# A replicating store in place of three loads, and the first tile in four pieces

## The chip, the core and the metric

The kernel runs on one core of a Trainium2 chip. The metric is the device time of one execution in microseconds (us); the median of three runs stands for it. A core has a matrix engine (TensorE, PE in the profile; its weight loads are listed apart as PEld), three engines for elementwise work (VectorE or DVE, ScalarE or ACT, GpSimd or POOL) and SyncE (SP), which here only issues DMAs. DMAs issued by SP, ACT and POOL move data between HBM and the on-chip memory (128 partitions). Engines run on their own and wait for each other through semaphores.

## The reference

One transformer block in bfloat16 with 2048 tokens of width 1024. First, attention in which each token looks at eight earlier tokens, two apart; then a gated MLP that also mixes tokens.

```python
def _A_ref(x, wqkv, wo):                 # H = 32 heads of 32, W = 8 positions, dil = 2
    qkv = (x @ wqkv).reshape(B, S, 3, H, Dh).transpose(2, 0, 3, 1, 4)
    q, k, v = qkv[0], qkv[1], qkv[2]
    idx = pos[:, None] - off[None, :]    # off = 0, 2, ..., 14; masked where below 0
    logits = einsum('bhsd,bhswd->bhsw', q, k[idx]) * scale
    attn = softmax(where(mask, logits, -1e9))
    o = einsum('bhsw,bhswd->bhsd', attn, v[idx])
    return o.transpose(0, 2, 1, 3).reshape(B, S, D) @ wo

def _B_ref(x, w_in, w_sp, b_sp, w_out):  # Fh = 1792
    z = gelu(x @ w_in)
    z1, z2 = z[..., :Fh], layernorm(z[..., Fh:])
    g = einsum('ts,bsf->btf', w_sp, z2) + b_sp[None, :, None]
    return (z1 * g) @ w_out

h = x + _A_ref(layernorm(x), wqkv, wo)
out = h + _B_ref(layernorm(h), w_in, w_sp, b_sp, w_out)
```

## The kernel before

Tokens are taken in four chunks of 512, each of four tiles of 128 rows. The order is: q, k and v of all chunks; attention of each chunk with the output projection and the second layer norm ("head"); the two halves of the MLP input (`b_z2`, `b_z1`); and a last phase with the token mixing (L912) and the output projection (L927).

**The start.** Tiles 0 and 1 of x are loaded at L220 to L222, each in a left half (columns 0 to 511) issued by SP and a right half issued by ACT. Then ACT issues the load of `csb`, the constants, which hold the identity matrix that the transposes multiply with; SP goes on with the eight 256 KB pieces of the q weights (`wsb[0]`, "wq" in the profile), with tiles 2 and 3 in between, and later tiles and weights. Eight semaphores serve the DMAs of SP and ACT in turn, so a DMA can be issued only when the one eight before it has landed. Meanwhile TensorE runs `NWARM` matmuls on zeros (L211), whose result nobody uses. Tile 0 then goes through VectorE's statistics (`stats`, L240: one instruction per half), a square root on ACT, a reciprocal and three pieces of normalisation (L272). TensorE transposes the pieces (`xpose`, L283), ACT copies them out of PSUM (L284), and `q_left` (L287) begins with the products of tile 0 and the first five pieces of wq. Tile 1 follows on the same engines, then tiles 2 and 3. From the products of k and v on (L439), TensorE's work is large matmuls alone.

**The order of work.** PE, ACT, DVE and POOL execute in an order fixed at build time: the class `Order` plays through operations with estimated costs and priorities and emits them as it would start them. SP's instructions are ordered by the framework, outside the hand-written order (but for the first loads, L217). Costs in the planner are not touched by the change, and the planner knows a spread as one DMA operation of 7.0 us (`dma_op(7.0, spread, [prev])`).

**Attention.** In `attention(c)` (L461), partitions hold head and sub-dimension (p = 4 h + j, with 32 heads h and four j), and eight sub-steps `dl` lie in the free dimension. VectorE forms q*k for the eight positions and adds them up; TensorE sums over j, which gives logits in a layout of partition (q, h): a quarter q of the 512 tokens and a head. The softmax is done in that layout and gives `st["attn"]`, [128, 8 positions, 128 tokens]. To weigh v, every weight must be on all four partitions of its head: the tile `st["AB"]`. For positions 0 to 3 this is done by TensorE with a 0/1 matrix (`pbm`, L581, then copies at L594). For positions 4 to 7, "the second weight group", it goes through HBM (`spread`, L573): SP stores `attn[:, 4:8]` into `att_d[c]` (L574), and then loads it four times (L576), once for each j, into the partitions j, j+4, j+8, ... of AB. The first load must wait until the store has landed; what SP has to issue next stands behind it.

VectorE then multiplies v by the weights: y and z (positions 0 and 1), oT and zz (2 and 3), at L610, and position 4 as `av_b` at L613, the first that reads the second group; positions 5 to 7 as `av_p`, with additions (L621). y+z and oT+zz are added by DMAs that POOL issues (`gather`, L627; "av_y" and "av_oT"). The last addition completes `av_oT`, which the output projection reads as TensorE's stationary operand (L684).

**Other transfers near the spread.** SP stores q, k and v of later chunks from staging tiles (`stg`, four buffers, L451). POOL loads k, q, v of the next chunk (L470) and the MLP weights (`win`, L369).

Of the kernel before, what the change touches and what calls it, by code (L numbers as in the profile page):

```python
# [11 lines left out]
BF16 = mybir.dt.bfloat16  # L12
# [8 lines left out]
P = 128  # L21
NT = S // P
CH = 512
NCH = S // CH
# [5 lines left out]
EPS = 1e-5  # L30
SCALE = DH ** -0.5
NEG = -1.0e9
NWARM = 11
ALONE = 5
XRB = 3
LMODE = (1, 1, 1, 1)
# [27 lines left out]
class Order:  # L64
# [6 lines left out]
    def add(self, eng, us, fn, deps=(), prio=5.0, lat=0.1, take=None, free=None, table=None):  # L71
        o = _Op()
        o.eng, o.us, o.fn, o.prio, o.lat, o.free, o.table = eng, us, fn, prio, lat, free, table
        o.take = (take,) if isinstance(take, str) else take or ()
        o.deps = [d if isinstance(d, tuple) else (d, d.lat) for d in deps if d is not None]
        o.start, o.end, o.n = None, None, len(self.ops)
        self.ops.append(o)
        return o
# [49 lines left out]
def kernel(  # L128
# [12 lines left out]
    nc = tc.nc  # L141
    V, A, T = nc.vector, nc.scalar, nc.tensor
    dma = nc.sync.dma_start
    dma_w = nc.gpsimd.dma_start
    x2d = A_x[0]
# [6 lines left out]
    dpool = ctx.enter_context(tc.tile_pool(name="dram", bufs=1, space=DRAM))  # L152
    qkv_d = [dpool.tile([P, DLO, S], BF16, name=f"qkv_d{i}") for i in range(3)]
    h_d = dpool.tile([S, D], BF16, name="h_d")
    att_d = [dpool.tile([P, CH], BF16, name=f"att_d{i}") for i in range(NCH)]
    z1_d = dpool.tile([NF, P, S], BF16, name="z1_d")
    z2_d = dpool.tile([S, FH], BF16, name="z2_d")

# [36 lines left out]
    xts = {}  # L195
    pairs = {}

    def x_slot(i):
        if i // 2 not in pairs:
            pairs[i // 2] = l1.tile([P, 2, D], BF16, name="xp", tag="x4k", bufs=4)  # L200
        xts[i] = pairs[i // 2][:, i % 2, :]

    def load_pair(k):
        x_slot(2 * k)
        x_slot(2 * k + 1)
        dma(pairs[k][:], x2d[2 * k * P:(2 * k + 2) * P, :].rearrange("(t p) d -> p t d", p=P))
# [3 lines left out]
    wps = ps_tp.tile([P, CH], FP32, name="wps", tag="t0")  # L210
    for _ in range(NWARM):  # L211
        T.matmul(wps[:], warm[:, 0:P], warm[:], start=True, stop=True)
# [4 lines left out]
    with tc.manual_schedule(engines={mybir.EngineType.SP}):  # L217
        for i in range(TPC):
            x_slot(i)
        for i in range(2):  # L220
            for q_, lo in ((nc.sync, 0), (nc.scalar, CH)):
                q_.dma_start(xts[i][:, lo:lo + CH], x2d[i * P:(i + 1) * P, lo:lo + CH])  # L222
        A.dma_start(csb[:], consts_d.ap()[:, :])
        for kt in range(KT):
            dma(wsb[0][:, kt, :], wq_view[:, kt, 0:D])
            if kt == 4:
                for i in (2, 3):
                    dma(xts[i], x2d[i * P:(i + 1) * P, :])
        load_pair(2)
        load_pair(3)  # L230
        dma(wsb[1][:], wq_view[:, :, D:2 * D])
        load_pair(4)
        load_pair(5)
        xl = att.tile([P, TPC, D], BF16, name="xl", tag="prod", bufs=2)
        dma(xl[:], x2d[3 * CH:4 * CH, :].rearrange("(t p) d -> p t d", p=P))
        for i in range(TPC):
            xts[3 * TPC + i] = xl[:, i, :]
        dma(wsb[2][:], wq_view[:, :, 2 * D:3 * D])
# [137 lines left out]
    def dma_op(us, fn, deps, lat=0.1, free=None):  # L376
        return add("DMA", us, fn, deps, lat=lat, free=free)
# [83 lines left out]
    def attention(c):  # L461
# [18 lines left out]
        st, parts, qs, pvs = {}, {}, [{} for _ in range(W_WIN)], {}  # L480
# [5 lines left out]
        for g in range(W_WIN // nw):  # L486
            adds = []
            for wi in range(nw):
                w = g * nw + wi
# [53 lines left out]
        for hw in range(2):  # L543
            ws = slice(4 * hw, 4 * hw + 4)
# [20 lines left out]
        for hw in range(2):  # L565
            ws = slice(4 * hw, 4 * hw + 4)
            def at(ws=ws, hw=hw):
                if hw == 0:
                    st["AB"] = att.tile([P, W_WIN, CH], BF16, name="AB", tag="part", bufs=2)
                V.tensor_tensor(st["attn"][:, ws, :], st["sme"][:, 1, ws, :], st["rinv"][:].unsqueeze(1).to_broadcast([P, 4, P]), op=ALU.mult)  # L570
            prev = add("DVE", 0.61, at, [prev], prio=3.0, lat=0.1, take="part" if hw == 0 else None, free="prod" if hw else None)
            if hw:
                def spread(ws=ws):  # L573
                    dma(att_d[c][:], st["attn"][:, ws, :].rearrange("p w s -> p (w s)"))  # L574
                    for j in range(4):
                        dma(st["AB"][j::4, 4:8, :], att_d[c][:].rearrange("(q h) n -> h q n", h=32))  # L576
                abs_[1, 0] = abs_[1, 1] = dma_op(7.0, spread, [prev])
                break
            wait = add("DMA", BSLACK, lambda: None, [prev])
            for sh in range(2):  # L580
                def pbm(sh=sh, ws=ws, hw=hw):  # L581
                    if sh == 0:
                        pb = ps_att.tile([P, 2, 4, P], FP32, name="pb", tag="L")
                    else:
                        pb = ps_acc.tile([P, 2, 4, P], FP32, name="pba", tag="acc")
                    st["pb", hw, sh] = pb
                    for j in range(2):
                        sq = 2 * sh + j
                        T.matmul(pb[:, j], B4[32 * sq:32 * sq + 32, :], st["attn"][32 * sq:32 * sq + 32, ws, :],  # L589
                                 start=True, stop=True, tile_position=(32 * sq, 0))  # L590
                pm = add("PE", 0.20, pbm, [wait], prio=1.0, take="acc" if sh else "L", lat=0.2)
                eng = "DVE" if (hw == 0 and sh == 1) else "ACT"
                def cp(sh=sh, ws=ws, hw=hw, eng=eng):
                    (V.tensor_copy if eng == "DVE" else A.copy)(  # L594
                        st["AB"][:, ws, sh * 256:(sh + 1) * 256].rearrange("p w (j s) -> p j w s", j=2), st["pb", hw, sh][:])
                abs_[hw, sh] = add(eng, 1.25 if eng == "DVE" else 0.91, cp, [pm], prio=1.0 if eng == "ACT" else 2.9,
                                   free="acc" if sh else "L", lat=0.15)
# [304 lines left out]
    for c in range(NCH):  # L902
        wspT = wspTs[c]
        zg = p2.tile([P, NF, CH], BF16, name="zg", tag="zg")
        for fp in range(NF // 2):
# [3 lines left out]
            for j in range(2):  # L909
                f = 2 * fp + j  # L910
# [8 lines left out]
        for il in range(TPC):  # L919
            i = c * TPC + il  # L920
# [52 lines left out]
```

## Time and profile before

| | |
|---|---|
| median of three runs | 723.3 us (723.22 to 723.41) |
| profiled execution | 723.34 us, span of its records 721.6 us |
| granted TensorE clock, mean over the span | 1.00 |
| DMA moved | 113.12 MB, 157 GB/s over the span |
| landing of the store `att_d` (128 KB) | 1.7 to 2.4 us after issue |
| landing of a load of AB (128 KB) | 2.5 to 8.0 us after issue, slowest in chunk 1 |

In the profile a line such as "L613 DVE TENSOR_TENSOR av_b<-vT,AB" names the kernel's line, the engine, the operation and the tiles written and read. Views used here are: the page (a summary of the span), the waits (who waited for whom), the chain (the work that ended last, followed back), the timeline (start, duration, instruction and in brackets the idle time before it with what ended it), the view of one tile, and the DMA view, which for any stretch of time gives each queue's packets, MB and share of the engines' time. Queue q1 carries what SP issues, q10 what ACT issues, q0 what POOL issues. "Landing" is the time from the start of a DMA's issue to its last semaphore update.

### The profile page before, as it was taken

What the parts mean: (1) busy time and instruction counts of PE and PEld (TensorE: products, weight loads), DVE (VectorE), ACT (ScalarE), POOL (GpSimd) and SP (SyncE); (2) the same over time, 40 slices, a digit from 0 to 9 for tenths busy, and PEclk for the clock granted to TensorE, in tenths of its full rate; (3) what the DMA queues carried; (4) which work ended last, traced back from release to release, by engine and by line L of the source; (5) the groups of instructions that cost most, each with busy time, mean ns of one, the idle gap of its engine ahead of it and who ended that gap; (6) DMA issues with size and microseconds to landing.
All of it is one profiled execution on the core that took longest, in us unless ns stands there. A gap on an engine that the chain in (4) does not pass through costs nothing.

```text
span 721.6 us, 8559 instructions
## 1 busy us (share of the span) xinstructions
PE 714.1 (99%) x3493; PEld 370.3 (51%) x3537; DVE 420.8 (58%) x470; ACT 217.7 (30%) x280; POOL 51.2 (7%) x61
## 2 busy tenths in 40 slices
PE   8999999999999999999999999999999999999998
PEld 7766665666545444445445444444444444444444
DVE  6899899999999799988951103222222222222222
ACT  4523432533348866738825420000000000000000
POOL 0100010012110111000204100000000000000000
PEclk9999999999999999999999999999999999999999
DMA  9964697389973594642849899163016411120002
GB/s 327 322 185 110 201 215 206 128 233 277 312 301 58 188 238 142 233 117 66 223 129 294 230 299 295 48 148 116 29 45 128 132 33 45 35 86 11 0 17 71
DMA packets 117590, 113.12 MB, mean 157 GB/s; under 512 B 68080, under 2 KB 95120, under 8 KB 117424
## 3 DMA queue, kind: packets, MB, share of 16 engines
q1 hardware_dynamic: 108528, 75.48, 35.7%
q0 software_dynamic: 8448, 36.64, 17.6%
q8 instruction: 27, 0.44, 0.3%
q10 hardware_dynamic: 576, 0.47, 0.2%
q14 instruction: 11, 0.09, 0.0%
HBM read 57.19 MB, written 31.26 MB: 123 GB/s over the span
## 4 chain that ended last, share of the span: by engine, by line
PE 98%; DMA 0%; DVE 0%; issue 0%; ACT 0%
PE acc L912 27%; PE acc L439 21%; PE acc L816 13%; PE acc L761 13%; PE acc L927 13%; PE acc L684 8%; PE acc L287 2%; DMA xp<-in_A_x_dram 0%; PE L L527 0%; PE tpt L283 0%; PE pb L589 0%; DVE bnst L242 0%; DVE xn L272 0%; DVE bnst L243 0%; PE tpa L283 0%
## 5 line engine op out<-in xcount | busy, mean ns | idle before, releaser
L912 PE MATMUL acc<-wspT,z2sb 128*128 128x512 bf16 x878 | 193.1, 379 | 0.9
L912 PEld LDWEIGHTS <-z2sb 128*128 128x128 bf16 x896 | 87.7, 98 | 105.7
L915 DVE TENSOR_TENSOR g<-acc,bB 128x1024 bf16<-128x1024 f32 x28 | 34.3, 1224 | 160.2 <-PE acc L912 127.9
L816 PE MATMUL acc<-hnT,win 128*128 128x512 bf16 x448 | 98.0, 379 | 0.0
L761 PE MATMUL acc<-win,hnT 128*128 128x512 bf16 (+1 forms) x501 | 97.4, 352 | 0.6
L761 PEld LDWEIGHTS <-hnT 128*128 128x128 bf16 x512 | 49.9, 98 | 47.5 <-issue 0.7
L497 DVE TENSOR_TENSOR prod<-qT,kT 128x4096 bf16<-128x4096 bf16 x32 | 72.4, 2283 | 0.0
L927 PEld LDWEIGHTS <-zg 128*128 128x128 bf16 x462 | 44.7, 98 | 52.4
L816 PEld LDWEIGHTS <-win 128*128 128x128 bf16 x448 | 43.7, 98 | 52.6 <-issue 0.7
L450 ACT CAST stg<-acc 128x1024 bf16<-128x1024 f32 x36 | 36.4, 1011 | 77.2 <-PE acc L439 66.4
L934 DVE TENSOR_TENSOR ot<-acc,hr 128x1024 bf16<-128x1024 f32 x15 | 18.4, 1225 | 69.4 <-PE acc L927 60.5
L927 PE MATMUL acc<-wout_a,zg 128*128 128x512 bf16 (+2 forms) x260 | 58.0, 373 | 0.3
L439 PE MATMUL acc<-xnT,wk 128*128 128x512 bf16 x256 | 56.5, 380 | 0.0
L439 PE MATMUL acc<-xnT,wv 128*128 128x512 bf16 x256 | 56.1, 380 | 0.0
L684 PE MATMUL acc<-wo_sb,av_oT 128*128 128x512 bf16 x250 | 55.6, 379 | 0.3
L439 PEld LDWEIGHTS <-wv 128*128 128x128 bf16 x256 | 36.7, 144 | 18.5 <-issue 0.2
L439 PEld LDWEIGHTS <-wk 128*128 128x128 bf16 x256 | 36.6, 144 | 18.7 <-issue 0.7
L927 PE MATMUL acc<-wout_b,zg 128*128 128x512 bf16 (+2 forms) x193 | 43.8, 373 | 0.2
L439 PE MATMUL acc<-xnT,wq 128*128 128x512 bf16 x192 | 42.1, 380 | 0.0
L684 PEld LDWEIGHTS <-av_oT 128*128 128x128 bf16 x256 | 25.0, 98 | 30.1
L822 ACT ACTIVATE z1s<-acc 128x1024 bf16<-128x1024 f32 x28 | 28.6, 1022 | 37.8 <-PE acc L816 33.5
L501 DVE TENSOR_TENSOR prod<-prod 128x2048 bf16<-128x2048 bf16 x32 | 38.4, 1217 | 0.1
(140 smaller groups left out, 562.1 us busy)
## 6 DMA issues: line engine op xcount, KB each, us to landing
qkv_d<-stg SPq DMA_DIRECT2D x36, 256.0 KB, 3.9
z_d<-z1s SPq DMA_DIRECT2D x28, 256.0 KB, 2.6
z1c<-z_d SPq DMA_DIRECT2D x28, 256.0 KB, 2.8
z_d<-u SPq DMA_DIRECT2D x12, 448.0 KB, 2.8
z2sb<-z_d POOLq DMA_DIRECT2D x12, 448.0 KB, 9.7
xr<-in_A_x_dram SPq DMA_DIRECT2D x16, 256.0 KB, 3.1
av_y<-av_z POOLq DMA_DIRECT2D x4, 1024.0 KB, 8.6
av_oT<-av_zz POOLq DMA_DIRECT2D x4, 1024.0 KB, 12.1
```

Of the source, the lines that this page charges most:

```text
L439: T.matmul(G[key][:, j, :].rearrange("p (a b) -> p a b", a=TPC), wv[:, kt, dl, :], xnT[c][:, :, kt, :], start=(kt == 0), stop=(kt == KT - 1))
L450: A.copy(stg[:], G[key][:])
L497: V.tensor_tensor(st["prod"][:], qT[:], kT[:, :, o:o + CH], op=ALU.mult)
L501: V.tensor_tensor(dst, p_[:, 0:4, :], p_[:, 4:8, :], op=ALU.add)
L684: T.matmul(st["acc", il][:, nh, :], oTs[c][:, dl, il * P:(il + 1) * P], wo_sb[:, dl, nh * CH:(nh + 1) * CH], start=(dl == 0), stop=(dl == ...
L761: T.matmul(accf[:, n0:n1], hnTs[c][:, il, kt, :], wins[hf][:, kt, n0:n1], start=(kt == 0), stop=(kt == KT - 1))
L816: T.matmul(G["accy", c, fp][:, j, :].rearrange("p (a b) -> p a b", a=TPC), wt[:, kt, f0 * P:(f0 + 1) * P], hnTs[c][:, :, kt, :], start=(kt ...
L822: A.activation(z1s[:], G["accy", c, fp][:], ACTF.Gelu_apprx_tanh)
L912: T.matmul(acc[:, j, :], z2sb[a][:, f * P:(f + 1) * P], wspT[:, a, :], start=(a == 0), stop=(a == NT - 1))
L915: V.tensor_tensor(g1[:], acc[:], bB[:, c * CH:(c + 1) * CH].unsqueeze(1).to_broadcast([P, 2, CH]), op=ALU.add)
L927: T.matmul(outs, zg[:, f, il * P:(il + 1) * P], wt[:, f0, lo:hi], start=(f == 0), stop=(f == NF - 1))
L934: V.tensor_tensor(ot[:], acc[:].rearrange("p a b -> p (a b)"), hr[:], op=ALU.add)
```

## The change

Three edits.

First, tile 0 of x is loaded in four pieces of 64 partitions by 512 columns: SP takes partitions 0 to 63 and ACT 64 to 127, both with the left columns first and then the right ones. Tile 1 is loaded whole, by one DMA on SP. `csb` is still ACT's third DMA, and the first piece of wq is SP's fourth where it was the third.

Second, one of the eleven matmuls on zeros is dropped.

Third, in `spread` the store writes each row four times: its source is read with a step of zero over a new dimension of four, and `att_d[c]` grows from [128, 512] to [128, 4, 512]. One load then fills positions 4 to 7 of AB on all 128 partitions, with the row of partition (h, j) taken from copy j of row h. So 128 KB stored and four loads of 128 KB become 512 KB stored and one load of 512 KB, all in rows of 1 KB.

```diff
-NWARM = 11
+NWARM = 10
...
-    att_d = [dpool.tile([P, CH], BF16, name=f"att_d{i}") for i in range(NCH)]
+    att_d = [dpool.tile([P, 4, CH], BF16, name=f"att_d{i}") for i in range(NCH)]
...
-        for i in range(2):
-            for q_, lo in ((nc.sync, 0), (nc.scalar, CH)):
-                q_.dma_start(xts[i][:, lo:lo + CH], x2d[i * P:(i + 1) * P, lo:lo + CH])
+        for lo in (0, CH):
+            for q_, p0 in ((nc.sync, 0), (nc.scalar, P // 2)):
+                q_.dma_start(xts[0][p0:p0 + P // 2, lo:lo + CH], x2d[p0:p0 + P // 2, lo:lo + CH])
+        dma(xts[1], x2d[P:2 * P, :])
         A.dma_start(csb[:], consts_d.ap()[:, :])
...
                 def spread(ws=ws):
-                    dma(att_d[c][:], st["attn"][:, ws, :].rearrange("p w s -> p (w s)"))
-                    for j in range(4):
-                        dma(st["AB"][j::4, 4:8, :], att_d[c][:].rearrange("(q h) n -> h q n", h=32))
+                    dma(att_d[c][:], st["attn"][:, ws, :].rearrange("p w s -> p (w s)").unsqueeze(1).to_broadcast([P, 4, CH]))
+                    dma(st["AB"][:, 4:8, :], att_d[c][:].rearrange("(q h) j n -> (h j) q n", h=32))
                 abs_[1, 0] = abs_[1, 1] = dma_op(7.0, spread, [prev])
```

## The prediction

> **What bounds the kernel now.** I read the page first (busy time and chain), then the waits of TensorE, the start in order of time, and last the stretch around the second attention, where the only wait on a tile of the change stands.
>
> The page, busy time and chain:
>
> ```profile
> span 721.6 us, 8559 instructions
> ...
> PE 714.1 (99%) x3493; PEld 370.3 (51%) x3537; DVE 420.8 (58%) x470; ACT 217.7 (30%) x280; POOL 51.2 (7%) x61
> ...
> PE 98%; DMA 0%; DVE 0%; issue 0%; ACT 0%
> ```
>
> The waits of TensorE alone (us in total, times, longest):
>
> ```profile
> PE wps L212 <- DVE eps_t L213: 1.2, 1, 1.2
> PE tpt L283 <- DVE xn L272: 1.0, 1, 1.0
> ```
>
> TensorE is busy without a pause; both of its waits lie in the first 6.3 us. In the chain, its pieces from 23.23 us to 718.65 follow each other at 10.74 us per 49 matmuls, 0.219 each. After the start there is nothing to win: a change there can only bring a wait. A gain can come from the first microseconds alone. The start in order of time (start, duration):
>
> ```profile
> 1.68 0.45 ACTq L223 DMA_DIRECT2D csb<-qt_consts  x1
> ...
> 3.57 0.69 DVE L242 BATCH_NORM_STATS2 bnst<-xp 128x6 f32<-128x512 bf16 x1 [2.27 <-DMA xp<-in_A_x_dram]
> ...
> 6.31 0.38 PE L283 MATMUL tpt<-csb,xn 128*128 128x128 bf16 x4 [0.99 <-DVE xn L272]
> ```
>
> The left half of tile 0 is there at 3.54 (issued 0.74, landed 2.8 later), and statistics, root, reciprocal and normalisation follow without a hole. The first piece of xn starts at 5.66 and takes 0.35: done 6.01. TensorE starts 0.3 later than that. The identity csb, issued at 1.68 and landing 4.5 later, arrives at 6.18: that is the last thing the first transpose waits for.
>
> VectorE in the second attention:
>
> ```profile
> 172.43 2.29 DVE L610 TENSOR_TENSOR av_zz<-vT,AB 128x4096 bf16<-128x4096 bf16 x1
> 175.53 2.29 DVE L613 TENSOR_TENSOR av_b<-vT,AB 128x4096 bf16<-128x4096 bf16 x1 [0.80 <-DMA AB<-att_d]
> ...
> 194.01 2.29 DVE L621 TENSOR_TENSOR av_oT<-av_oT,av_b 128x4096 bf16<-128x4096 bf16 x1
> ```
>
> TensorE at the same place:
>
> ```profile
> 196.59 1.68 PE L684 MATMUL acc<-wo_sb,av_oT 128*128 128x512 bf16 x7
> ```
>
> av_b already waits 0.8 us for the spread weights, and from there to the end of av_oT at 196.30 VectorE has no hole. TensorE takes av_oT at 196.59: 0.28 us of slack. The same slack is 0.94 in the first attention (114.82 to 115.76), 0.62 in the third and 1.5 in the fourth; and AB is there before av_b needs it by 1.5 us in the first (92.6 against 94.04), 4.1 in the third (254.0, 258.1) and 5.1 in the fourth. So the second attention decides.
>
> **The change part by part.**
>
> *The first tile.* Two 128 KB loads (left on SP, right on ScalarE's queue) become four of 64 KB; the left columns are first on both queues. Issues cost 0.4 us each, and the first are still at 0.74. Ahead of the left half's last byte lie 128 KB instead of up to 256. Between 2 and 4 us the DMA moved 298 GB/s, so 128 KB less is 0.44 us. Against it: the left half now also waits for ScalarE's queue, whose first load landed 0.2 later (3.0 against 2.8 after issue). I take 0.44 - 0.2, about 0.25 us gained; bounds -0.2 (no saving, ScalarE's queue late) and +0.44. csb comes third on its queue as before but with 128 KB less ahead of it, some 0.4 earlier (5.75), so it stops binding: the first transpose would be at 6.06 - 0.25 = 5.81. That extra does not last, since the transposes of tile 1 at 9.06 wait for VectorE, which moves by 0.25 only. From 10.13 TensorE is dense and carries 0.25.
> The Trainium skill, "SBUF — State Buffer", section "Can I just issue two DMAs to hit both halves?", speaks against this part: two DMAs on the two partition halves share the same engines and gain about nothing over one. By that the landing, and the sum, would be 0.25 us later. No run here shows it yet; what I count is the order of columns, not the halves.
>
> *Tile 1* becomes one 256 KB load, third on SP. VectorE wants it at 6.5 and had it at 4.3; even 0.9 us (256 KB at 298 GB/s) later it is covered. The wq loads move one SP issue (0.43) back: the first landed at 5.96, its weight load is at 6.82; with the start 0.25 earlier some 0.2 us of cover remain. If that is gone it costs the rest of 0.25.
>
> *One warm-up matmul less.* The last ran from 4.94 and TensorE idled 1 us after it. It is off the path: nothing.
>
> *The spread.* Removed: three of four loads, each 0.6 us of SP issue. Added: the store writes four copies, 512 KB instead of 128, in rows of 1 KB: 512 packets instead of 128. The load moves the same 512 packets, in one DMA that waits for the whole store. In the third and fourth attention the 384 added packets take 1 to 2 us (at 746 packets in 2 us, or half of it) and the 4 and 5 us of cover hold. In the first, POOL's load runs only until 89; the store would end there at the latest, the load from 90.5 to 92 at 373 packets per us, landing by 94: the 1.5 us and the 0.94 hold.
>
> In the second the store meets POOL's load of win and then the adding DMA av_y. The DMA view, cut to 164.6-165.5, 165.5-167, 167-172, 172-174.5 and 175-179 (queue 1 is SP's, queue 0 POOL's):
>
> ```profile
> q1 hardware_dynamic: 147, 0.13, 57.4%
> ...
> q0 software_dynamic: 58, 0.24, 69.5%
> ...
> q1 hardware_dynamic: 346, 0.34, 19.2%
> ...
> q1 hardware_dynamic: 663, 0.61, 71.9%
> ...
> q1 hardware_dynamic: 184, 0.18, 16.1%
> ```
>
> SP's queue got 69 packets per us beside win, 265 when win was ending, 46 beside av_y. Of the store's 512 packets 131 would be out by 165.5 (147 less 16 semaphore writes). The 381 left: at 69 per us until 171.0; or, if the 30% free engine time of 165.5-167 serves them (0.305 x 1.5 us x 373 = 171), until 170.0. I take 170.5. From last packet to landing: 0.5 us for the store now (165.4, 165.9), 1.8 for the last AB load (its 768th packet of the stretch falls at 172 + 422/265 = 173.6, landing 175.4); I take 1.2: 171.7. From issue to first packet: 0.8 for the store now (163.9, 164.7); over 2.4 for the staging store issued at 83.75, of which 5 packets moved in 84.6-86.2; I take 1.6: 173.3. Then 1.2 us x 265 = 318 packets until 174.5, and the 194 left at 46 per us: 178.7; landing 179.9. That is 4.5 us after today's 175.4. Less the 0.28 of slack, TensorE waits 4.2 us at 196.6.
> Behind the waiting load on SP's queue stand the staging stores of 168.8 and 171.7; their four buffers and three PSUM accumulators (two more of 3.45 us each) hide that: nothing. SP's order is not written by hand and may shift with three issues fewer per attention (1.8 us of issue time); SP idles between stores, so I count nothing, and if a store moved ahead of the load it would be 256 packets, 1 to 4 us, which the range holds.
>
> The sum goes against the profiled execution, 723.34 us (its span of 721.6 and 1.8 around it), which stands at the median of 723.3: 723.34 - 0.25 + 4.2 = **727.3 us**. It is steep: until 174.5 each 0.1 us costs 0.6 later, because 265 packets per us become 46.
>
> **The rivals.**
> *The store gets stuck (B).* The staging store of 164.36 got nothing before 167 (one packet in 165.5-167). If the store's rest does as it did: 167 + 381/69 = 172.5, landing 173.7, load from 175.3 at 46 per us for 11.1 us, landing 187.6: 12.2 late, less 0.28: 735.0. For it: that row. Against: the store is 0.5 us ahead of POOL's stream, the staging store was behind it.
> *The spread is hidden (C, not slower).* If the store keeps the rate of 83.5-84.1 (120 in 0.6 us, 200 per us) past POOL's start it lands by 168, and the load lines up behind the staging store's 256 packets with no hole, as the four do now: AB near 175.4 again, 723.34 - 0.25 = 723.1. It decides at a landing of the store by about 169. For it: queue 0 moved only 58 packets in 165.5-167. If the halves bring nothing, 723.3.
> *The clock.* The warm-up weight loads are 0.43 us apart until 4.15 while a matmul later takes 0.22: TensorE begins at half rate for some 3 us. Slow again after a long wait, it would lose up to 1.5 us, on top of the forecast 728.8; a wait of 1.15 us before 6.31 did not do it.
> The Trainium skill, "TensorE: Matmul & The Clock Gate", Part 1, puts the fall back to half clock at an idle window of about 3.4 us; no stretch of this trace is long enough to show it.
> *Faster by over 0.2%* would need 1.4 us out of a start that has 0.44 to give.
>
> **How the numbers follow.** 0.2% is 1.4 us, about what a measurement here can tell from no change. Forecast, 724.8 to 730: 0.40. B, 730 to 736: 0.27. Clock or another late transfer, slower as well: 0.03. C, 722.7 to 724.7: 0.28. Faster: 0.02. So slower 0.70, same 0.28, faster 0.02. Likeliest 727.3, its own range 724.8 to 730; eight in ten from 722.7 (C) to 735.0 (B at its worked-out price).
>
> **What would show it.** The first statistics at 3.3 instead of 3.57 and the first transpose near 5.8: the start. The landing of the 512 KB store (171.7 forecast, under 169 in C, over 173 in B) and the wait of av_b for AB in the second attention (0.8 now, 5.3 forecast), with a new wait of TensorE's L684 on av_oT. If av_b waits under 1.1 us, the prediction is wrong and C right. If L684 waits in the first attention too, I have undersized the store there.

## The result and the profile after

The changed kernel takes 732.5 us (median of four runs, 731.7 to 734.4) against 723.26; the ratio is 1.0127, 95% interval 1.0108 to 1.0146. It is 9.2 us slower where 4.0 were forecast. The profiled execution took 732.77 us with a span of 730.9, which is 9.3 longer than before. The page of the changed kernel:

```profile
span 730.9 us, 8582 instructions
...
PE 720.2 (99%) x3536; PEld 371.2 (51%) x3536; DVE 420.9 (58%) x470; ACT 217.8 (30%) x280; POOL 51.0 (7%) x61
...
PEclk9999999999989999999999999999999999999999
...
PE 92%; DVE 4%; DMA 3%; SPq 1%; ACT 0%; issue 0%
```

The span is longer, and TensorE is still shown busy 99% of it; that share is too coarse to tell a wait of a few microseconds from matmuls that take longer. One slice of the clock line (the 12th, 201 to 219 us) has an 8 between the nines, so some matmuls there were slower. The chain now has 4% of VectorE and 3% of DMA in it, where it had 0%. The waits of TensorE after, followed by the wait of `av_b` from the list of VectorE (us in total, times, longest):

```profile
PE acc L684 <- DVE av_oT L621: 5.7, 1, 5.7
PE wps L212 <- DVE eps_t L213: 1.2, 1, 1.2
PE acc L288 <- DMA wq<-in_A_wqkv_dram: 0.4, 1, 0.4
PE tpt L284 <- DVE xn L273: 0.3, 1, 0.3
...
DVE av_b L613 <- DMA AB<-att_d: 6.8, 1, 6.8
```

The new wait stands where the prediction put it, at the second attention, once, for `av_oT`. It is 5.7 us and not 4.2. The chain of work in the second attention shows what ended last (start, duration):

```profile
164.51 9.36 DMA att_d<-attn
173.87 0.02 SPq L576
...
173.93 8.24 DMA AB<-att_d
...
182.19 2.29 DVE av_b L613
```

The store of four copies took 9.4 us and the single load behind it 8.2. From `av_b` on, VectorE runs without a hole to the end of `av_oT` at 202.97, as before the change, so the whole delay reaches TensorE.

What follows the wait costs as well. Busy time in windows of the trace after the change (window, length, then busy us and instructions of PE, PEld, DVE, ACT, POOL, the granted clock, DMA share, GB/s):

```profile
190.00:197.00 7.00, 7.00 (x37) 3.75 (x36) 6.90 (x4) 3.04 (x4) 2.49 (x3) 1.00 1.03 358
197.00:203.10 6.10, 0.45 (x4) 0.08 (x2) 6.03 (x4) 1.39 (x3) 0.17 (x1) 0.88 1.03 398
203.10:208.60 5.50, 5.50 (x14) 1.88 (x15) 4.27 (x2) 0.00 (x0) 0.00 (x0) 0.51 0.99 371
```

The last of these windows in the trace of before:

```profile
203.10:208.60 5.50, 5.50 (x27) 2.51 (x26) 5.16 (x9) 1.34 (x3) 0.00 (x0) 1.00 1.01 376
```

After the wait the granted clock is 0.51 for 5.5 us: 14 matmuls fit where 27 did. They follow each other at 0.427 us instead of 0.216, and 14 x 0.21 = 2.9 us are lost.

The third part is the start. The first matmul of the first logits (L527 before, L528 after) is the first fixed point behind it: 74.96 before, 75.58 after, so +0.62. The sum is 0.62 + 5.8 (the gap on TensorE between the starts of the matmuls on either side, less the usual distance; the wait list, which goes by ends, has 5.7) + 2.9 = 9.3 us: the whole difference between these two profiled executions.

**Where the store was.** The DMA view after the change, cut to 164.6-165.5, 165.5-167, 167-172, 172-174.5, 174.5-178 and 178-182.5 us (queue, packets, MB, share of the engines; q1 is SP's, q0 POOL's):

```profile
q1 hardware_dynamic: 26, 0.02, 7.8%
...
q0 software_dynamic: 26, 0.11, 65.8%
...
q0 software_dynamic: 404, 1.65, 82.8%
q1 hardware_dynamic: 358, 0.37, 20.6%
...
q0 software_dynamic: 132, 0.48, 61.0%
q1 hardware_dynamic: 442, 0.42, 47.9%
...
q0 software_dynamic: 181, 0.74, 109.2%
...
q0 software_dynamic: 93, 0.32, 52.0%
q1 hardware_dynamic: 802, 0.79, 50.9%
```

The store was issued at 164.51. The 26 packets of SP's queue before 165.5 are the tail of the staging store ahead of it; between 165.5 and 167 SP's queue moved nothing. POOL's load of `win`, issued at 164.16, has its first packets in the trace at 165.75. The store's first come at 167.26; it then gets 72 packets per us until 172 and the rest when `win` thins out, and lands at 173.87. A staging store issued at 165.15 stands between the store and the load on SP's queue: of the 442 packets from 172 to 174.5, 154 are the store's last, 256 the staging store's, and 32 are the 16 packets of 4 bytes that end each of the two. So the load, issued at 173.93, has none of them. It gets nothing at all until 178, beside the adding DMA av_y, and most of its packets in the gap between av_y and the next adding DMA. It lands at 182.17.

### The profile page after: what moved, and what is told of

Its sections match the earlier page's. It is cut to its first block, busy times and chain, and to the rows that moved or that the text cites. A ratio compares the mean times of both kernels' runs of the same rounds, so it can differ in the third digit from the quotient of the medians.

```text
span 730.9 us, 8582 instructions
## 1 busy us (share of the span) xinstructions
PE 720.2 (99%) x3536; PEld 371.2 (51%) x3536; DVE 420.9 (58%) x470; ACT 217.8 (30%) x280; POOL 51.0 (7%) x61
## 4 chain that ended last, share of the span: by engine, by line
PE 92%; DVE 4%; DMA 3%; SPq 1%; ACT 0%; issue 0%
PE acc L912 26%; PE acc L440 16%; PE acc L816 13%; PE acc L927 13%; PE acc L761 13%; PE acc L684 8%; PE acc L288 2%; DMA att_d<-attn 1%; DVE av_b L621 1%; DMA AB<-att_d 1%; DVE av_p L613 1%; DMA wq<-in_A_wqkv_dram 1%; DVE av_oT L621 0%; DVE av_b L613 0%; PE L L528 0%; SPq L226 0%
## 5 line engine op out<-in xcount | busy, mean ns | idle before, releaser
L684 PE MATMUL acc<-wo_sb,av_oT 128*128 128x512 bf16 x256 | 58.6, 392 | 5.7 <-DVE av_oT L621 5.7
L684 PEld LDWEIGHTS <-av_oT 128*128 128x128 bf16 x256 | 25.6, 100 | 38.0 <-DVE av_oT L621 6.0
```

The costliest lines, as they stand in the source:

```text
L684: T.matmul(st["acc", il][:, nh, :], oTs[c][:, dl, il * P:(il + 1) * P], wo_sb[:, dl, nh * CH:(nh + 1) * CH], start=(dl == 0), stop=(dl == ...
```

## The experiments

Ten kernels were run, in three groups, each beside the kernel before on the same chip (its medians there 723.62, 723.85 and 723.38 us). The ratios, with their 95% intervals, use all runs and not the medians alone, so they differ a little from the quotient of the two medians. The theory after the result: in the second attention the store of four copies loses the engines to the `win` load, everything else follows from the late load of AB, and the start adds little. The rivals: the later start is the cause; not the store but the single load is; TensorE's waits, not its clock, carry the loss; a store of 512 packets is slow whatever it meets.

**The spread alone** (the kernel before with the new `spread` and the larger `att_d`; start and warm-up as before).

> The spread alone (store of four copies, one load), first tile and warm-up as before. Theory: the spread in the second attention carries the loss but for the start's 0.6 us: store landed near 173.5, load landed near 181.5, VectorE waits some 6.8 us for it, TensorE some 5.8 us for av_oT, and then runs at half clock for some 6.8 us, which costs 2.9: 723.3 + 8.7 = 732.0, between 730.5 and 734. Rival: the later start of the changed kernel is what moves the store behind POOL's load; with the start as before the store would land by 168 and the time stay under 725.

Measured: 732.59 us (731.2 to 734.9), ratio 1.0116 [1.0087, 1.0145]. The waits of TensorE, and the two DMAs in the view of `att_d` (issue time, start):

```profile
PE acc L683 <- DVE av_oT L620: 5.4, 1, 5.4
...
L574 SPq DMA_DIRECT2D att_d<-attn x1: 553/553/553, 163.7 to 163.7; - x1
L575 SPq DMA_DIRECT2D AB<-att_d x1: 359/359/359, 173.2 to 173.2; - x1
```

The spread alone carries the loss. Here the store was issued 0.8 us earlier than in the full change (163.73), POOL's load 0.8 earlier too (163.37), and the store landed just as late (9.4 us after issue). The later start is not the cause.

**The start alone** (four pieces, tile 1 whole, ten warm-up matmuls) **and the pieces alone** (the same with eleven).

```diff
-            for q_, lo in ((nc.sync, 0), (nc.scalar, CH)):
-                q_.dma_start(xts[i][:, lo:lo + CH], ...)
+        (the two loops of the change, then dma(xts[1], x2d[P:2 * P, :]))
```

> The first tile in four pieces, tile 1 in one load and ten warm-up matmuls; the spread as before. Theory: the loss of 0.6 us at the start comes from wq's fifth piece landing 1.2 us later, half of which is the later issue of SP (first wq issue at 2.9 instead of 1.67) and repeats, half slow packets that need not: 723.5 to 724.0. Rival: the start is worth the 0.25 us that was forecast, 723.0, and the 0.6 of the profiled execution was chance.

> The first tile in four pieces and tile 1 in one load, eleven warm-up matmuls. In four profiled executions with the old loads TensorE's first matmul on the logits (the first instruction at L527) begins at 74.8 to 75.1; with the new ones at 75.6 and 76.3. Theory: the loads do this, with SP's first wq issue at 2.9 instead of 1.67: 75.5 to 76.4 here too, and wq's or tile 2's landing as a new wait. Rival: the missing warm-up matmul does it: 74.8 to 75.1 here.

Measured: 723.91 us, ratio 0.9998 [0.9986, 1.0010], and 723.80, ratio 0.9993 [0.9983, 1.0002]. Neither can be told from the kernel before, and both intervals also hold the gain of 0.25 us (0.03%) that was forecast, so only the traces speak on it. In the profiled runs the first logits matmul stands at 76.30 and 75.34; the second lies between what the theory (75.5 to 76.4) and its rival (74.8 to 75.1) had expected, and settles neither. The timeline of the pieces alone shows why nothing is gained (start, duration):

```profile
0.74 1.48 SPq L222 DMA_DIRECT2D xp<-in_A_x_dram  x2
0.75 1.21 ACTq L222 DMA_DIRECT2D xp<-in_A_x_dram  x2
1.99 0.60 ACTq L224 DMA_DIRECT2D csb<-qt_consts  x1
2.27 0.59 SPq L223 DMA_DIRECT2D xp<-in_A_x_dram  x1
2.91 2.32 SPq L226 DMA_DIRECT2D wq<-in_A_wqkv_dram  x5
```

The pieces did what was meant for the data: the left ones landed at 2.93 and 3.16 (before: 3.55). But an issue of a piece takes 0.6 to 0.8 us where a half of tile 0 took 0.4, so the first load of wq is issued at 2.91 and not at 1.67. TensorE then waits for wq, 0.4 us in the changed kernel, and the later tiles and pieces of wq come about 1.2 us later.

**Which DMA of the spread.** Two kernels separate the store from the load. One stores four copies and loads four times, each from its own copy; the other keeps the 128 KB store and reads it with one load of 512 KB, whose source has a step of zero over the four. This second kernel leaves out the spreading to heads, so its weights are the wrong ones and it serves for its time alone.

```diff
 (four copies, four loads)
+  dma(att_d[c][:], st["attn"][:, ws, :]...unsqueeze(1).to_broadcast([P, 4, CH]))
+  for j in range(4):
+      dma(st["AB"][j::4, 4:8, :], att_d[c][:, j, :].rearrange("(q h) n -> h q n", h=32))
 (small store, one load)
   dma(att_d[c][:], st["attn"][:, ws, :].rearrange("p w s -> p (w s)"))
+  dma(st["AB"][:, 4:8, :], att_d[c][:].unsqueeze(1).to_broadcast([P, 4, CH]))
```

> The store writes four copies (512 packets), but four loads fetch them as before, each from its own copy. Theory (the store's size is the cause): the store lands near 173.5 as in the changed kernel, the last load a little later than one load would, at 182 to 185: 731 to 736. Rival (the single large load is the cause: it has to begin in the adding DMA's stream): the four loads go as before and the time stays within 1 us of 723.3.

> The store is the old one of 128 KB; one load fetches 512 KB from it, reading each of its rows four times (a source with step zero over the position). It leaves the spreading to heads out, so the weights are the wrong ones; packets and bytes of the load are those of the changed kernel. Theory (store's size): the store lands near 166 as before, the load follows behind the staging store, landing near 175.4 or sooner: 723.0 to 723.6. Rival (the single load): VectorE waits 5 us or more at av_b, 730 or more.

Measured: 737.98 us, ratio 1.0188 [1.0165, 1.0211], with the large store, and 724.18, ratio 1.0005 [0.9989, 1.0022], with the small one (somewhat above the expected 723.0 to 723.6, as is the kernel before on that chip). Of the kernel with the small store, the view of `att_d` and the wait of `av_b`:

```profile
L574 SPq DMA_DIRECT2D att_d<-attn x1: 332/332/332, 164.0 to 164.0; - x1
L575 SPq DMA_DIRECT2D AB<-att_d x1: 359/359/359, 166.0 to 166.0; - x1
...
DVE av_b L612 <- DMA AB<-att_d: 0.5, 1, 0.5
```

The single load of 512 KB is innocent: behind a store that has landed by 165.9 it is there at 175.3, as the four were. With the large store the four loads did worse than the one (the last landed at 187.4, and the time lies above the expected range): they sit behind each other and miss the gap that the single load caught. TensorE waits twice there, 5.1 us because the staging buffers run out (its L439, for the copy at L450) and 4.6 us for `av_oT`, and runs at half clock for 6.8 us after each. So the store's size is what loses.

**Which attention.** The old spread in chunk 1 only, the new one in the other three.

```diff
+  if c == 1:
+      (the 128 KB store and the four loads of before)
+      return
   (the store of four copies and the single load)
```

> The store of four copies and one load in the first, third and fourth attention, the old store and four loads in the second. Theory: the second attention alone carries the loss, where POOL's load of the MLP weights begins 0.1 us before the large store's first packet: 723.2 to 723.9, no wait of TensorE for av_oT. Rival: every attention pays some of it: 725 or more.

Measured: 724.07 us, ratio 1.0003 [0.9994, 1.0012]; TensorE has no wait after the start. The time is just above the expected 723.2 to 723.9, but the kernel before stands at 723.85 there, and no difference between the two can be told. The loss is all in the second attention, and the other three new spreads cost nothing that could be measured.

**The clock.** The new spread, with 26 matmuls of 512 columns, whose result is overwritten, ahead of the first L684 of chunk 1, so that TensorE stays busy while it would wait.

```diff
+  if c == 1 and il == 0:
+      for _ in range(26):
+          T.matmul(st["acc", il][:, 0, :], wo_sb[:, 0, 0:P], wo_sb[:, 0, 0:CH], start=True, stop=True)
```

> The spread alone, and 26 more matmuls on the output weights, whose result is overwritten, in front of the second chunk's output projection, where TensorE waits for av_oT (26 times 0.216 is 5.6 us of a wait of 5.4 to 5.8). Theory: of the 9 us that the spread costs, 5.5 are the wait and 2.9 the half clock after it; the filled wait keeps the clock, and the time falls by 2.9 against the spread alone, 732.4 to 729.5 (728.5 to 730.5). Rival: the slow matmuls come from something else that happens there (DMA traffic, the reading of av_oT), and the time stays at 732.

Measured: 730.98 us (729.4 to 731.9), ratio 1.0087 [1.0065, 1.0108]. The windows around the place, from its trace:

```profile
198.80:204.50 5.70, 5.65 (x28) 2.60 (x28) 5.63 (x4) 1.55 (x3) 0.00 (x0) 1.00 1.02 394
204.50:210.00 5.50, 5.50 (x27) 2.54 (x27) 5.50 (x5) 0.06 (x1) 0.00 (x0) 1.00 1.04 396
```

The clock stays at 1.00 and 27 matmuls fit into the 5.5 us behind the place, where the changed kernel had 14: what the half clock cost is gone in the trace. In the time the kernel is 1.6 us below the spread alone, less than the 2.9 and just above the expected 728.5 to 730.5, and the two intervals (1.0087 to 1.0145 and 1.0065 to 1.0108) overlap. So the size of the clock's part rests on the traces: the granted clock over the span is 1.000 in three of the four runs here, and 0.993 to 0.998 in all four of the spread alone. In this profiled run csb landed at 7.34, which put its start 2.3 us later; its span is therefore no measure of the gain.

**Who is first.** Two kernels move the `win` load behind the store: one waits for the store's landing; the other is the whole change with one GpSimd instruction ahead of the load, which delays its issue by 1.2 us.

```diff
 (behind the landing)
+  w_ = load_win(0, ...)        # issued in spread of chunk 1, after the store
+  tc.add_manual_dep(w_.ins, s_.ins.name, wait_for, ...)
 (delayed)
+  if k == 0:
+      nc.gpsimd.memset(t[:, 0, :], 0.0)
   dma_w(t[:], win_view[:, :, c0:c0 + wd])
```

> The spread alone, but in the second attention POOL's load of the first MLP weights waits until the store has landed. Theory (the order in which the two streams begin decides): the store's first packet comes 1.1 us after its issue, it lands at about 167, as in the third and fourth attention 3.2 us after issue, the load of AB lands before 175, TensorE does not wait: 723.2 to 724.0. Rival (the store is slow beside the staging stores or for its size alone): landing after 170, 728 or more.

> The whole change, with one GpSimd instruction put ahead of the weight load (L370, win0): it writes zeros over the first 1,024 columns of the tile that the load then fills, so it waits for the same TensorE instruction as the load and delays the load's issue by its own duration, which no row shows (about 1 us is assumed). In the changed kernel the load was issued at 164.16, 0.35 us ahead of the store, and its packets came at 165.5, 0.1 us ahead of where the store's first were due. Theory (of the two streams the one that begins first holds the engines; the store was late by one tenth of a microsecond): the store's packets now come first, at about 165.6, it lands by 168.5, the single load is then beside the weight load's stream and lands between 174 and 177.5, av_b waits 0 to 2 us, TensorE waits for av_oT at most 2 us and keeps its clock, and the time is 723.4 to 726.0. Rival (a store of 512 packets beside a weight load is slow in whatever order they begin): the store lands after 171, and the time is above 728. If the wait of av_b is gone and the time is still above 724.5, what is late next is the second weight load, as in the kernel in which the first waited for the store's landing.

Measured behind the landing: 727.5 us (725.4 to 728.4), ratio 1.0039 [1.0022, 1.0056]. The landings in the view of `att_d` (shortest, median, longest of store and load), and TensorE's first wait:

```profile
DMA to landing us min/median/max: 3.3/3.7/4.1
...
PE acc L764 <- DMA win<-in_B_w_in_dram: 2.3, 1, 2.3
```

Without the other stream the store takes 3.3 us and the load 4.1; AB is there at 172.2, earlier than in the kernel before, and `av_b` waits for nothing. But the loss has moved: the first `win` load is issued at 168.7 instead of 163.5, the adding DMAs behind it on POOL's queue land later (av_y at 187.2 instead of 181.8), and so does the second `win` load, at 198.0 (193.4 before; 0.9 us of the difference is the later start of this profiled run), and TensorE waits 2.3 us for it at 195.8. That wait did not lower the clock. The expected 723.2 to 724.0 was wrong, because I followed AB and not what stands behind the load that I had moved.

Measured with the delay: 734.29 us (733.9 to 734.8), ratio 1.0149 [1.0133, 1.0164]. The view of `att_d`, then the waits of VectorE and TensorE:

```profile
L577 SPq DMA_DIRECT2D att_d<-attn x1: 549/549/549, 164.8 to 164.8; - x1
L578 SPq DMA_DIRECT2D AB<-att_d x1: 360/360/360, 168.2 to 168.2; - x1
...
DMA to landing us min/median/max: 3.3/9.7/16.1
...
DVE av_b L615 <- DMA AB<-att_d: 8.7, 1, 8.7
...
PE acc L686 <- DVE av_oT L623: 4.9, 1, 4.9
PE acc L442 <- ACT stg L453: 2.1, 1, 2.1
```

The DMA view of this kernel from 165.9 to 168.2 us has only SP's queue (packets, MB, share of the engines):

```profile
q1 hardware_dynamic: 671, 0.67, 95.7%
```

The time misses the expected 723.4 to 726.0 by far, but the store's part of the theory holds. POOL's load was issued 0.66 us behind the store (165.44 against 164.78) instead of 0.35 ahead of it, and the same store, of the same size and from the same place, lands 3.3 us after its issue instead of 9.4. The part on the load fell: it was now behind `win`, then beside av_y, and landed 16.1 us after its issue, at 184.3 instead of the 174 to 177.5 expected. A staging store behind it landed at 189.8, and the staging buffers, which I had costed at nothing, ran out (the wait of L442). So the order decides who loses, not whether something is lost.

**Another start.** The kernel before with csb issued ahead of the second half of tile 1.

```diff
+            if i == 0:
+                A.dma_start(csb[:], consts_d.ap()[:, :])
-        A.dma_start(csb[:], consts_d.ap()[:, :])
```

> The kernel before, with the load of the constants (csb) issued on ScalarE's queue ahead of the second half of x tile 1 instead of behind it; nothing else. In profiled runs with the old loads csb landed anywhere from 5.4 to 7.3 us and the first transpose followed by 0.1 to 0.5 us; with the pieces, where csb is issued about 1 us ahead of the first load of wq, it landed at 4.2 to 4.7. Theory (csb, landing behind the first load of wq, sets the first transpose, and nothing at the start binds as hard behind it): csb lands before 5.0, the first transpose starts when its rows are normalised, at 5.9 to 6.1, the first logits matmul (L527) starts at 74.5 to 74.9 where it was 74.96, and the time is 0.1 to 0.6 us under the kernel before. Rival (wq and the tiles behind it take over at once): the first transpose is earlier but L527 is not, and the time is within 0.2% of the kernel before.

Measured: 723.48 us against 723.38, ratio 0.9999 [0.9990, 1.0007]. csb landed at 4.27 and the first transpose started at 5.99 (before: 6.31), but the displaced half of tile 1 landed at 6.53 (4.33) and the first logits matmul stands at 75.24. The rival holds: the tiles and wq take over at once. No version here beats the kernel before.

## Why the prediction was wrong in size

**Where and why, right.** Second attention, `av_b`, `av_oT`, L684: the wait came where it was forecast, in one place, and none in the first, third and fourth. That three spreads are free was shown by leaving only those in. One warm-up matmul less did nothing that could be measured.

**The store, wrong.** The step was "131 would be out by 165.5", with the rest from there at 69 per us. The sum took the first packet at 0.8 us after issue, as for the 128 KB store. The large store has its first packet 1.2 us after issue in the two kernels where nothing is in its way here (issued 164.84 and 164.78, first packets at 166.05 and 165.98), and so it does in the first, third and fourth attention. In the changed kernel that would be 165.7, the moment in which `win` begins (165.75), and none of its packets was out by 167. The same tie, within 0.1 us, stands in the three other kernels in which the large store met `win` as it was (the spread alone, the four loads, the filled wait), and the store lost each time, landing 9.4 us after issue. The 72 per us from then on agree with the 69 that I had taken. This is rival B in its mechanism. That its landing came out too (173.7 worked out, 173.87 measured) is partly luck: B had 381 packets left at 167 where all 512 were, and `win` thinned out at 173 and let the last of them through (361 packets of SP's queue from 173 to 174.5). The row against B, "the store is 0.5 us ahead of POOL's stream", held for the small store only: it came from that store's first packets, and 0.4 us of longer preparation used the lead up.

**The load, wrong in kind.** I gave it 318 packets before 174.5 and 46 per us beside av_y. It had none before 174.5: the staging store's 256 packets stood ahead of it on the queue, and the sum had left them out. It moved at none until 178, and then SP's queue moved 178 per us in a gap between two adding DMAs (802 packets in 4.5 us, the load's 512 and a staging store's 256 among them) that the calculation did not have. The errors against each other gave 182.2: later than the 179.9 forecast, and earlier than B's 187.6. So the wait was 5.7 us where 4.2 stood in the sum, and that it was no further off is partly luck.

**The clock, left out of the sum.** It stood among the rivals with a price of "up to 1.5 us". It cost 2.9, because the half clock lasted 6.8 us by the trace's clock record (201.69 to 208.51) and not 3. The Trainium skill, "TensorE: Matmul & The Clock Gate", Part 1, has a fall to half clock after an idle window of about 3.4 us; the trace now agrees, since 5.7 us brought it here, and in the kernel with four loads waits of 4.6 and 5.1 did, each for 6.8 us. No run has a wait of 4.2 us, but it is close enough to the 4.6 that the forecast should have had the term in the sum.

**The start, wrong in its issues.** "Issues cost 0.4 us each" is the step: the pieces cost 0.6 to 0.8. The step "some 0.2 us of cover remain" for wq fell with it; the first load of wq moved back by 1.2 us, not 0.43. In the profile that is +0.62 where -0.25 was forecast; in the time of the kernel with the start alone no difference can be seen, so neither sign is shown, and profiled starts of one and the same code differ by more than 2 us (csb landing at 5.4 to 7.3, the first logits matmul at 74.8 to 77.2). The data itself moved as meant: the left pieces landed at 3.09 and 3.31, the first statistics began at 3.41 (3.57 before, 3.3 forecast), csb landed at 4.30 (5.75 forecast) and the first transpose began at 5.97 (6.31 before, 5.81 forecast). In these traces what was gained there is lost again to the late wq.

The differences add up: +0.9 at the start, +1.5 in the wait, +2.9 by the clock make 5.3, and 727.3 + 5.3 = 732.6, beside 732.77 for the profiled execution. The term left out, the clock, is the largest of the three.

## What to carry to other kernels

Fewer DMAs are not cheaper where the next stream is already on its way: compare when the first packets come, for the DMA as it will be and not as it was, and follow a load through each stretch in which another stream is running. A wait that a change brings to TensorE should be costed with the clock behind it: here 5.7 us of waiting took another 2.9. And moving a transfer out of the way moves what stands behind it on its queue, which is to be costed in the same way.

## What was not expected of the hardware

- A DMA on SP's queue that is issued while POOL's queue is running can get no packets at all for a while: 1.5 us beside the start of `win` (165.5 to 167), 3.5 us beside av_y (174.5 to 178; if the load needs the store's 1.2 us from issue to first packet, the stretch up to 175.1 is its own). In the first attention of the changed kernel it was the other way round: the store, issued 83.37, had its packets from 84.5 to 86.4, and POOL's load of kT, issued at 83.61, began at 86.25, 2.6 us after issue where the kernel before has 1.6. The Trainium skill, "DMA: Bandwidth & Descriptors", section "Queues, rings and completion order", has each engine go round between the queues that have work, packet by packet; by that SP's queue should have had a share in both stretches, and in these traces it had none. What keeps it out, the preparation of its packets or the engines themselves, no run here shows.
- A smaller DMA can be dearer to issue: a load of 64 partitions by 512 columns took 0.57 to 0.81 us in the changed kernel, one of 128 partitions by 512 columns, with twice the bytes, 0.40 to 0.46 in the kernel before.
- In the records of the changed kernel the stretch at full clock before the fall lasted 194.56 us, 57 times 3.413, and the half clock 6.83, twice that. The clock seems to change only on a grid of 3.413 us. A stretch of the grid need not be idle throughout for the fall: in the kernel with the delayed `win` the clock fell at 202.88, and of the 3.41 us before it TensorE idled only the last 2.6 (its matmuls ended at 200.26). A wait of 2.3 us in mid-kernel was free of it; in one profiled run a gap of the same length at the start brought one period at half clock (7.63 to 11.05).
